# Modulation gates through DRAM, DMA transposes and idle products in a fused adaLN block of sliding attention and SwiGLU

## The chip, the core and the metric

One core of a Trainium2 chip. The metric is device time of one execution in microseconds (us), lower is better. The kernel before takes 255.45 us in the median of the four runs made beside the changed kernel (254.44 to 256.28), and 254.8 to 255.2 us in the calls of the experiments. The calls fell on different chips; in each, the kernel before was run beside the experiments. Most executions agree within a few tenths of a per cent; a run counts as "slow" when it is over 1.5% above the fastest of the same kernel. Ratios use the fast runs alone. Differences in us are of medians of all runs, and where slow runs shift one, the text says so. A kernel that was looked at only once has the state "unknown".

## The reference

A transformer block of 2048 rows by 512 columns, in bf16, whose two branches are modulated by a condition vector `c`:

```python
mod = (silu(c) @ w_mod)                        # six vectors of 512: sa, ca, ga, sb, cb, gb
h = layernorm(x) * (1 + ca) + sa               # LN1
x = x + ga * attention(h, wqkv, wo)            # 32 heads of 16; 8 keys, 2 rows apart, looking back
h = layernorm(x) * (1 + cb) + sb               # LN2
x = x + gb * ((silu(h @ w1) * (h @ w3)) @ w2)  # hidden size 1792
```

`ga` and `gb` are called the gates. Each is a row of 512 numbers that multiplies the columns of an output. The kernel multiplies them into the weights `wo` and `w2` once.

## The kernel before

The program is a list of operations. Each has an engine, an estimated cost and a priority; a planner in the host program places them in time by these, which fixes the order on every engine, and semaphore waits are then derived from the data. **Engines work strictly in that order.** The numbers in the priority table were found by search over the planner's estimates. The rows are handled in 16 tiles of 128. Parts that the change touches:

```python
# the condition vector times one, as four 128x128 stationary tiles (all columns equal)
for t in range(KT):
    p.op("dve", lambda e, t=t: e.tensor_scalar(csb[:, t, :], ones[:], csT[:, t:t + 1], None, op0=ALU.mult), 180, k, ...)

def gate(i):
    def mm(e):                       # the product comes out already repeated in all 128 partitions
        for t in range(KT):
            ins = e.matmul(bank(vm), csb[:, t, :], wm_g[i][:, t, :], start=(t == 0), stop=(t == KT - 1))
        return ins
    p.op("pe", mm, 4 * MM, k, r=[vwmg[i], vcsb] + wm_hold, w=[vm])
    dst = (ga_bc, gb_bc)[i]
    p.op("act", lambda e: e.activation(dst[:], bank(vm), ACT.Copy), c_act(512), k, r=[vm], w=[vg[i]])

def ln_stats(which, T):              # which = 0: LN1, 1: LN2
    ...                              # statistics on VectorE, 1/sqrt on GpSimd (add, then power)
    p.op("dve", lambda e: e.tensor_scalar(vn.at[:], x_sb[:, T, :], mv[:, i, 0:1], rs[:, i, :], op0=ALU.subtract,
                                          op1=ALU.mult), 350, ("nm", i), r=[vx[T], vr, vm], w=[vn])

def ln_T(which, gi, vns):            # a group of two or four tiles: transposed by TensorE into PSUM ...
    ...
    ins = e.transpose(b[:, col:col + P], vns[tt].at[:, ft * P:(ft + 1) * P], ident[:])
    ...                              # ... and scaled and shifted by ScalarE on the way out of PSUM
    return e.activation(vh.at[:, ft, 0:n * P], b[:, j * 512:j * 512 + n * P], ACT.Identity, bias=..., scale=...)

def values(T, i, ve, va):            # attention weights of a tile: written to DRAM, read back in another layout
    p.dma(bass.AP(a_dram, ...), lambda: ve.at[0][:, i]..., ("ad", T), 65536, ...)       # from SyncE
    p.dma(lambda: val.at[:], bass.AP(a_dram, ...), ("al", T), 65536 * 3, ...)           # from SyncE
    ...
```

The five LN2 groups feed the FFN: tiles 0 and 1, then three groups of four, then tiles 14 and 15.

The softmax here doesn't subtract the row's maximum and nothing guards it: scores larger than these inputs give would overflow.

## Time and profile before

| | before |
|---|---|
| time, median | 255.45 us |
| span of the profiled execution | 253.2 us |
| TensorE busy | 239.0 us (94%) |
| VectorE busy | 191.7 us (76%) |
| ScalarE busy | 111.4 us (44%) |
| GpSimd busy | 32.0 us (13%) |

In the profile, L with a number is a line of the kernel's source, and "out<-in" are the tiles by the program's names: `pall` is PSUM, `sb_wm_g` the gate weights, `sb_w` the FFN weights, `sb_vsh` the shifted values of the attention, `sb_xn` a normalized tile, `sb_h` a transposed group. The three views that carry the argument (engine totals and slices, busy time by stage, the chain that ended last) are shown and read in the prediction. The table of DMA issues of the kernel before (destination and source, issuing queue, number, size of each, median us from issue to landing):

```profile
sb_w<-in_B_w_dram SPq DMA_DIRECT2D x4, 512.0 KB, 7.9
...
a_scratch_dram<-sb_attn SPq DMA_DIRECT2D x16, 64.0 KB, 2.5
sb_al<-a_scratch_dram SPq DMA_DIRECT2D x16, 64.0 KB, 2.5
```

Loads of 512 KB land after about 8 us, the attention weights after 2.5 us. TensorE's table of waits is headed by these two (what was waited for, total us, how often, the longest), and the others are 1.3 us or less:

```profile
PE pall L574 <- DVE sb_xn L558: 6.4, 2, 5.6
PE pall L522 <- DMA sb_wm_s<-in_w_mod_dram: 1.5, 1, 1.5
```

Both are in the head of the kernel. After that TensorE hardly waits at all.

### The profile page before, as it was taken

The page shows a single profiled execution, that of the slowest core. Times are in us where ns is not written, and L with a number is a line of the kernel's source. Part 1 is how long each engine was busy: PE and PEld are TensorE (multiplying, and loading weights), DVE is VectorE, ACT ScalarE, POOL GpSimd, SP SyncE. Part 2 cuts the span into 40 slices and gives each one's busy share as a digit, 9 for nine tenths or more (in the row PEclk, how much of TensorE's full clock was granted, in tenths as well). Part 3 has the DMA queues.
Part 4 walks back from the last instruction along what each step waited for, and adds up shares of the span by engine and source line. Part 5 has one row for each costly group of instructions (what it writes and reads, how often), then busy time and mean ns, then how long its engine had stood idle before and what let it go on. Part 6 is the DMA issues. An engine that isn't in the chain of part 4 may idle for free.

```text
span 253.2 us, 5473 instructions
## 1 busy us (share of the span) xinstructions
PE 239.0 (94%) x2262; PEld 140.4 (55%) x2296; DVE 191.7 (76%) x298; ACT 111.4 (44%) x198; POOL 32.0 (13%) x81
## 2 busy tenths in 40 slices
PE   0599989999999999999999999999999999999995
PEld 0367555655488666546654544556544444565562
DVE  4759889999998989999899899999952443432432
ACT  2159748864863347432462273334234322420120
POOL 6237641001000040000002200020030000000000
PEclk9999999999999999999999999999999999999999
DMA  6997999899954595322369145393001000000101
GB/s 193 359 324 189 293 350 331 210 331 284 241 123 140 142 310 196 64 31 62 106 194 295 54 104 85 87 310 103 4 0 44 0 0 21 21 3 21 41 23 41
DMA packets 45817, 36.29 MB, mean 143 GB/s; under 512 B 19408, under 2 KB 36576, under 8 KB 45792
## 3 DMA queue, kind: packets, MB, share of 16 engines
q1 hardware_dynamic: 45264, 35.94, 49.4%
q8 instruction: 18, 0.29, 0.5%
q10 hardware_dynamic: 528, 0.00, 0.1%
q14 instruction: 7, 0.06, 0.1%
HBM read 30.67 MB, written 5.26 MB: 142 GB/s over the span
## 4 chain that ended last, share of the span: by engine, by line
PE 87%; DVE 5%; DMA 2%; POOL 2%; issue 1%; SPq 0%; ACT 0%; DVEq 0%
PE pall L771 36%; PE pall L792 19%; PE pall L615 9%; PE pall L755 5%; PE pall L742 5%; PE pall L633 5%; PE pall L673 4%; PE pall L574 2%; DMA sb_x<-in_A_x_dram 2%; POOL sb_rs L555 1%; DVE sb_xn L558 1%; DVE sb_st L550 1%; POOL sb_rs L553 1%; DVE sb_pq L664 1%; DVE sb_hh L780 1%
## 5 line engine op out<-in xcount | busy, mean ns | idle before, releaser
L771 PE MATMUL pall<-sb_h,sb_w 128*128 128x512 bf16 (+1 forms) x548 | 100.0, 336 | 0.7
L771 PEld LDWEIGHTS pall<-sb_h,sb_w 128*128 128x128 bf16 x560 | 53.7, 97 | 41.4
L777 ACT ACTIVATE sb_sg<-pall 128x512 bf16<-128x512 f32 (+1 forms) x70 | 35.6, 511 | 70.6 <-PE pall L771 70.3
L780 DVE TENSOR_TENSOR sb_hh<-sb_sg,pall 128x512 bf16<-128x512 bf16 (+1 forms) x70 | 39.5, 577 | 26.0 <-PE pall L771 23.8
L792 PE MATMUL pall<-sb_w,sb_hh 128*128 128x512 bf16 x216 | 49.7, 379 | 0.4
L664 DVE TENSOR_TENSOR sb_pq<-sb_q,sb_kT 128x4096 bf16<-128x4096 bf16 x16 | 36.4, 2283 | 0.5 <-ACT sb_q L622 0.3
L792 PEld LDWEIGHTS pall<-sb_w,sb_hh 128*128 128x128 bf16 x224 | 21.4, 98 | 23.5 <-DVE sb_hh L780 0.2
L615 PE MATMUL pall<-sb_h,sb_wqkv 128*128 128x512 bf16 (+1 forms) x155 | 31.9, 344 | 0.3
L582 ACT ACTIVATE sb_h<-pall,sb_modc 128x512 bf16<-128x512 bf16 (+1 forms) x36 | 23.1, 708 | 18.7 <-PE pall L574 13.1
L553 POOL TENSOR_TENSOR sb_rs<-sb_mv,sb_cst 128x1 f32<-128x1 f32 x32 | 8.8, 276 | 151.4 <-DVE sb_mv L551 148.4
L733 DVE TENSOR_TENSOR sb_vsh<-sb_vsh,sb_al 128x4096 bf16<-128x4096 bf16 x12 | 27.3, 2285 | 0.4 <-DMA sb_vsh<-v_scratch_dram 0.4
L798 DVE TENSOR_TENSOR sb_o<-pall,sb_x 128x512 bf16<-128x512 f32 x16 | 11.0, 688 | 18.0 <-PE pall L792 18.0
L550 DVE BATCH_NORM_STATS2 sb_st<-sb_x 128x6 f32<-128x512 bf16 x32 | 21.8, 682 | 3.3 <-DMA sb_x<-in_A_x_dram 3.2
L555 POOL TENSOR_TENSOR sb_rs<-sb_rs,sb_cst 128x1 f32<-128x1 f32 x32 | 20.9, 654 | 2.5
L615 PEld LDWEIGHTS pall<-sb_h,sb_wqkv 128*128 128x128 bf16 x160 | 15.1, 101 | 11.0 <-ACT sb_h L582 0.7
L633 PE MATMUL pall<-sb_wqkv,sb_h 128*128 128x512 bf16 x63 | 17.6, 411 | 1.5 <-DVE sb_xn L558 1.3
L574 PE MATMUL pall<-sb_ident,sb_xn 128*128 128x128 bf16 x128 | 12.8, 227 | 6.4 <-DVE sb_xn L558 6.4
L673 PEld LDWEIGHTS pall<-sb_E,sb_pq 128*128 128x128 bf16 x512 | 14.7, 96 | 2.7 <-DVE sb_pq L664 0.6
L748 ACT ACTIVATE sb_ot<-pall 128x512 bf16<-128x512 f32 x16 | 9.6, 598 | 13.6 <-PE pall L742 13.6
L574 PEld LDWEIGHTS pall<-sb_ident,sb_xn 128*128 128x128 bf16 x128 | 9.5, 101 | 10.6 <-DVE sb_xn L558 6.9
L755 PE MATMUL pall<-sb_wo,sb_ot 128*128 128x512 bf16 x58 | 15.0, 379 | 0.3
L673 PE MATMUL pall<-sb_E,sb_pq 128*128 128x32 bf16 x512 | 15.1, 177 | 0.0
(59 smaller groups left out, 163.8 us busy)
## 6 DMA issues: line engine op xcount, KB each, us to landing
sb_vsh<-v_scratch_dram SPq DMA_DIRECT2D x48, 256.0 KB, 4.4
sb_vshx<-v_scratch_dram SPq DMA_DIRECT2D x16, 256.0 KB, 4.5
sb_wm_s<-in_w_mod_dram SPq DMA_DIRECT2D x2, 1024.0 KB, 6.6
v_scratch_dram<-sb_v SPq DMA_DIRECT2D x16, 128.0 KB, 5.0
sb_w<-in_B_w_dram SPq DMA_DIRECT2D x4, 512.0 KB, 7.9
out_dram<-sb_o SPq DMA_DIRECT2D x16, 128.0 KB, 1.7
sb_w<-in_B_w_dram SPq DMA_DIRECT2D x1, 1792.0 KB, 8.9
sb_wqkv<-in_A_wqkv_dram SPq DMA_DIRECT2D x3, 512.0 KB, 7.9
```

Of the source, the lines that this page charges most:

```text
L550: o = p.op("dve", lambda e: e.bn_stats(st[:, i, :], x_sb[:, T, :]), 670, k, r=[vx[T]], w=[vs])
L574: ins = e.transpose(b[:, col:col + P], vns[tt].at[:, ft * P:(ft + 1) * P], ident[:])
L615: ins = e.matmul(bank(vp)[:, 0:n], wqkv[:, t, col:col + P], vh.at[:, t, 0:n], start=(t == 0), stop=(t == KT - 1))
L633: ins = e.matmul(bank(vp), vh.at[:, t, tt * P:(tt + 1) * P], wqkv[:, t, 2 * D:3 * D], start=(t == 0), stop=(t == KT - 1))
L664: return e.tensor_tensor(vp.at[:], in0, in1, ALU.mult)
L673: ins = e.matmul(b[:, c0:c0 + H], vp.at[:, w, ft, :], E_sb[:, ft, :], start=(ft == 0), stop=(ft == KT - 1))
L733: return e.tensor_tensor(v_w, v_w, a_w, ALU.mult)
L755: ins = e.matmul(bank(vy), vt.at[:, ft, :], wo[:, ft, :], start=(ft == 0), stop=(ft == KT - 1))
L771: ins = e.matmul(bank(vp)[:, 0:n], wt[:, t, fi * P:(fi + 1) * P], vh.at[:, t, 0:n], start=(t == 0), stop=(t == KT - 1))
L777: p.op("act", lambda e: e.activation(vt.at[:, 0:n], bank(vgp)[:, 0:n], ACT.Silu), c_act(n), k, r=[vgp], w=[vt], table="silu")
L780: p.op("dve", lambda e: e.tensor_tensor(vh_.at[:, 0:n], vt.at[:, 0:n], bank(vup)[:, 0:n], ALU.mult), c_dve(n), k, r=[vt, vup], w=[vh_])
L792: ins = e.matmul(bank(vz), vhh[fi].at[:, tt * P:(tt + 1) * P], w2[:, fi, :], start=(fi == 0), stop=(fi == NF - 1))
```

## The change

The intent: TensorE is the bound, so take work off it, and relieve VectorE, its nearest rival.

- The gates are computed as 16 one-column products each. The result is a column spread over partitions, which a GpSimd DMA writes to DRAM as a row of 512 numbers and a second one reads back, repeated over all partitions.
- LN2 groups 1 to 4 (14 tiles) are transposed by DMA rather than by TensorE; ScalarE then scales and shifts in place.
- LN2's normalization goes from VectorE to ScalarE, for which GpSimd computes a bias with two small products per tile.
- The DMAs of the attention weights are issued by GpSimd instead of SyncE.
- 70 idle products of 128 columns run at the start, to warm the array.
- The outputs of tiles 14 and 15 are done in halves of 256 columns.
- The priorities were searched again, with new cost estimates; the first loads are ordered differently.

```diff
+    def warm(i):
+        def mm(e):
+            for _ in range(5):
+                ins = e.matmul(bank(vw)[:, 0:P], ones[:], ones[:], start=True, stop=True)
+        p.op("pe", mm, 535, ("warm", i), r=[vc], w=[vw])          # NWARM = 14 of them
 ...
     def gate(i):
         def mm(e):
-            for t in range(KT):
-                ins = e.matmul(bank(vm), csb[:, t, :], wm_g[i][:, t, :], start=(t == 0), stop=(t == KT - 1))
+            for j in range(4):
+                for t in range(KT):
+                    ins = e.matmul(b[:, j:j + 1], wm_g[i][:, t, j * P:(j + 1) * P], csT_bf[:, t:t + 1], start=(t == 0),
+                                   stop=(t == KT - 1))
-        p.op("pe", mm, 4 * MM, k, r=[vwmg[i], vcsb] + wm_hold, w=[vm])
+        p.op("pe", mm, 16 * 27, k, r=[vwmg[i], vcs] + wm_hold, w=[vm])
+        p.op("dve", lambda e: e.tensor_copy(gcol[:, 4 * i:4 * i + 4], bank(vm)[:, 0:4]), 180, k, r=[vm], w=[vgc])
+        p.dma(bass.AP(g_dram, i * D, [[1, P], [P, KT]]), bass.AP(gcol, 4 * i, [[8, P], [1, 4]]), k, 90000, r=[vgc], w=[vgd], eng="pool", cost=900)
         dst = (ga_bc, gb_bc)[i]
-        p.op("act", lambda e: e.activation(dst[:], bank(vm), ACT.Copy), c_act(512), k, r=[vm], w=[vg[i]])
+        p.dma(dst[:], bass.AP(g_dram, i * D, [[0, P], [1, D]]), k, 131072, r=[vgd], w=[vg[i]], eng="pool", cost=900)
 ...
     def ln_stats(which, T):
+        if which:
+            p.op("pool", lambda e: e.tensor_tensor(nb[:, T, :], mv[:, i, 0:1], cst[:, 2:3], ALU.mult), 200, ...)
+            p.op("pool", lambda e: e.tensor_tensor(nb[:, T, :], nb[:, T, :], rs[:, i, :], ALU.mult), 200, ...)
+            p.op("act", lambda e: e.activation(vn.at[:], x_sb[:, T, :], ACT.Identity, bias=nb[:, T, :], scale=rs[:, i, :]),
+                 c_act(512) + 50, ("nm", i), r=[vx[T], vr, vb], w=[vn])
+            return vn
 ...
     def ln_T(which, gi, vns):
+        if which and gi >= DMA_T:                                  # DMA_T = 1
+            for tt in range(n):
+                p.dma(lambda tt=tt: vh.at[:, :, tt * P:(tt + 1) * P], lambda tt=tt: vns[tt].at[:], k, 157000, r=[vns[tt]],
+                      part=[vt, vh], cost=1250, transpose=True)
+            for ft in range(KT):
+                ... e.activation(vh.at[:, ft, 0:n * P], vh.at[:, ft, 0:n * P], ACT.Identity, bias=..., scale=...)
+            return vh
 ...
     def values(T, i, ve, va):                                      # both attention-weight DMAs
-              ("ad", T), 65536, r=[va, ve], w=[vad], cost=400)
+              ("ad", T), 65536, r=[va, ve], w=[vad], cost=900, eng="pool")
 ...
     def ffn_w2(T, tt, vhh):
+        if T >= NT - 2:                                            # two halves of 256 columns, each stored by itself
 ...
+    for i in range(NWARM):
+        warm(i)
 ...   (a wholly new table of priorities)
```

## The prediction

> **What bounds the kernel now.** I read the engine totals first, then the slices, then a table of busy time by stage, and last the chain that ended last at its two ends.
>
> ```profile
> PE 239.0 (94%) x2262; PEld 140.4 (55%) x2296; DVE 191.7 (76%) x298; ACT 111.4 (44%) x198; POOL 32.0 (13%) x81
> ...
> PE   0599989999999999999999999999999999999995
> ...
> DVE  4759889999998989999899899999952443432432
> ...
> PE 87%; DVE 5%; DMA 2%; POOL 2%; issue 1%; SPq 0%; ACT 0%; DVEq 0%
> ```
>
> TensorE works almost without a break from the second slice to the last, and 87% of the chain that ended last is TensorE. VectorE is a near second until 180 us and then only half busy. By stages (columns: length, then busy time and instruction count of PE, PEld, DVE, ACT, POOL, then granted clock, DMA share, GB/s):
>
> ```profile
> 0.00:12.00 12.00, 3.54 (x44) 2.13 (x45) 7.55 (x26) 2.51 (x4) 5.39 (x25) 1.00 0.83 273
> 18.00:30.00 12.00, 11.75 (x93) 8.01 (x94) 11.04 (x23) 10.56 (x24) 8.31 (x14) 1.00 0.88 225
> 30.00:60.00 30.00, 28.87 (x402) 17.30 (x406) 28.61 (x37) 21.03 (x36) 3.52 (x5) 1.00 0.99 308
> ...
> 240.00:253.20 13.20, 10.25 (x66) 6.29 (x65) 3.91 (x8) 1.92 (x5) 0.00 (x0) 1.00 0.09 31
> ```
>
> TensorE's idle time is 8.46 us in the first 12 us and 2.95 us after 240; summed over all windows between (12 to 240 us) it is only about 2.7 us. So a microsecond of matmul taken off between 12 and 250 us is worth about a microsecond of the end, as long as its feeders keep up. The head is a chain of its own (start, duration, what):
>
> ```profile
> 7.99 0.70 DVE sb_st L550
> ...
> 9.43 0.73 DVE sb_h L589 x2
> 10.16 0.33 DVE sb_xn L558
> 10.51 3.59 PE pall L633 x8
> 14.10 0.85 PE pall L615 x4
> 14.95 0.21 PE pall L574 x2
> 15.16 0.85 PE pall L615 x4
> 16.02 0.21 PE pall L574 x2
> 16.23 1.40 PE pall L615 x12
> 17.63 0.22 PE pall L574 x4
> ```
>
> The eight 512-column products from 10.51 take 449 ns each and the 256-column ones 213 ns; from 16.23 on the latter take 117 ns and later 109. TensorE runs at half speed until about 16.2 us although the granted clock in the slices reads 9 or more all along: this is the slow start of a rested array, which that row does not show.
>
> **What the Trainium skill says.** (1) "TensorE: Matmul & The Clock Gate", Part 1: a rested array runs at half clock and needs about 3.4 us of sustained activity, seen by a free-running window; start to start 426.7 ns cold and 215.7 warm at 512 columns, 106.7 and 55.6 at 128, and never below about 25 ns. The trace agrees: 449 (with a start delay) and 213 for half as many columns while cold, 55 ns for a warm transpose (0.22 us for four), and 0.79 us for the 32 one-column products of the second modulation, 24.7 ns each. (2) "DMA: Bandwidth & Descriptors", DMA Transpose (X-bar): the plain transpose can be issued only by the two hardware queues, and its rules say a transpose beside ordinary DMAs needs nothing extra. No run here shows it yet. The changed kernel issues all of them from SyncE, so from one stream. (3) "GPSIMD Engine Reference", Specifications: GpSimd's way to SBUF is shared with VectorE, with contention under two-input instructions. The trace agrees: the power on 128x1 elements takes 0.55 us in the median and 2.70 us once, when VectorE runs its 2.28 us product of two tensors. (4) The DMA page, SWDGE vs HWDGE vs iDMA: descriptors of a GpSimd DMA are written by GpSimd into SBUF, so the same lock-out delays them; the trace of before has no such DMA.
>
> **The change part by part.**
>
> *Transposes.* LN2 groups 1 to 4 (14 of 16 tiles) are transposed by DMA. That removes 14 x 4 = 56 TensorE transposes of 55 ns: 3.08 us, all on TensorE's saturated stretch. In their place come 14 DMAs of 128 KB from SyncE; the diff reckons 1.25 us of issue each. The evictions of these groups (ScalarE, 772 ns in the median form, from PSUM) become ScalarE passes in SBUF of about the same size. The latency of such a group grows: a four-tile group needs four issues plus a landing (2.5 us is what small DMAs took before), about 7 us instead of about 1. A preceding FFN group has 112 x 216 + 56 x 216 ns = 36 us of products, so this can be hidden.
>
> *Gates.* Two gates of four 512-column products (4 x 215.7 = 0.86 us each) become 16 one-column products at 24.7 ns, 0.40 us each. TensorE saves 2 x 0.47 = 0.94 us. The two 0.6 us ScalarE copies and the 1.0 us of VectorE broadcast go; two dependent DMAs per gate come, off the path, since the scaling of wo and w2 has tens of microseconds of slack.
>
> *Idle products first.* 14 x 5 products of 128 columns run from about 1.3 us, when the ones tile is set. Cold they take 70 x 107 ns = 7.5 us, less once the clock rises; that is two windows of activity, so TensorE should be warm when the first projection starts. The work between 10.51 and 16.23 is then 8 x 216 + 8 x 109 + 4 x 55 ns = 2.82 us instead of 5.72: 2.90 us saved at most.
>
> *Tail.* The last two tiles' outputs are cut into halves of 256 columns. The last VectorE add goes from 0.69 us to about 0.42 (what a 256-column product from PSUM takes on VectorE here, 419 ns), and the last store is half as large. Against that 56 x 109 ns for 28 x 215.7 ns, +0.07 us. Net about 0.25 us.
>
> *Off the bound.* VectorE loses 16 LN2 scalings of 0.40 us (6.5 us), now on ScalarE at about 0.6 us (+9.6 us of a 44% engine). One more half of an LN1 eviction goes from VectorE to ScalarE (+1.1 us there). The 32 attention-weight DMAs leave SyncE (0.58 and 0.38 us of issue each) for GpSimd. I credit nothing directly; VectorE at 95% until 180 us becomes less of a second bound, and that lets the saving on TensorE reach the end.
>
> Sum before debits: 3.08 + 0.94 + 2.90 + 0.25 = 7.2 us.
>
> **Debits.** (a) First loads: by the new priorities both pairs of x tiles go ahead of the modulation weights and another 512 KB of x ahead of the value weights. About the same bytes as before have to land before modulation (1.5 MB), so the first projection starts at 10.5 to 11 us, but the value weights may land 1.5 us later than before (512 KB at the 350 GB/s of that stretch). I take 0.4 us. (b) ScalarE in the first stage: from 9.43 to 30 us it worked 14.6 of 20.6 us, and 88% between 18 and 30. With 1.1 us more work in 2.9 us less time it is at 89% over the stretch; with eight PSUM banks as buffer some of the warm start is lost again. I take 0.6 us. (c) The array may not be warm in time or may pause too long while it waits for the modulation weights: 0.3 us on average. (d) New waits of ScalarE behind transposed tiles or of VectorE behind GpSimd DMAs: 0.4 us. (e) In return the order was searched anew, and some of the 2.7 us of idle time inside may go: I count 0.6 us. Together 7.2 - 1.7 + 0.6 = 6.1 us. From 255.89 us that is 249.8; I put it at **249.7 us** (2.4% less).
>
> **The rivals.** *ScalarE becomes the first-stage bound.* For: the 88% above, and two-tile groups need about 6.5 us of ScalarE evictions (eight of 0.39, two of 0.60, four of 0.56) for 5.6 us of warm TensorE work. Against: from 30 us on ScalarE is idle a third of the time. The warm start would then bring about 1 us and the time be 251.5. *Attention weights come late.* For: GpSimd can be held up to 2.3 us per VectorE product, twice in a row per tile (write, then read back), where SyncE needed 2.5 + 2.5 us to landing. Against: VectorE has other products to do meanwhile, and several tiles are in flight; FFN products fill TensorE after 70 us. If it fails, VectorE idles 1 to 2 us a tile for a few tiles: 252 to 254 us. *A transposed group is late*, so that ScalarE, which works in order, holds up SiLU and with it TensorE: 1 to 2 us per group at worst, 252 us. *All is hidden well and the new order removes most inner idle time:* 247.5.
>
> **Range and chances.** The three TensorE savings are firm in size (4.0 us without the warm start); only the 2.9 us of the warm start and the new waits vary. The saving must exceed 5.1 us for more than 2%. I expect 6.1 with a spread of some 2 us: range 247.0 to 252.6, chance of over 2% faster 0.70, within 2% 0.28, slower 0.02.
>
> **What would show it.** TensorE's busy sum without the idle products falls by about 7 us, of which 3.1 by transposes (72 left of 128) and 0.9 by gates. The first value projections take 216 ns each, not 449, starting at 10.5 to 11 us. If they are still at 427 ns, or ScalarE is over 95% between 12 and 30 us, step three fails. TensorE's idle time between 12 and 240 us stays under 4 us; if it is over 6, a wait took the place of the work removed, and the table of waits would name the transposed tiles or the attention weights. The last add is a 256-column one, and the span after the last product is about 2.6 us instead of 2.9. VectorE's total falls to about 183 us and ScalarE's rises to about 120; if VectorE then idles before its attention products, the GpSimd route is to blame.

## More of the kernel before

In the gate's write the DRAM pattern `[[1, P], [P, KT]]` says: partition p puts its four numbers at positions p, p+128, p+256 and p+384. So one write of 1 KB is made of 512 pieces of two bytes, and pieces from neighbouring partitions lie side by side.

## The result, and the profile after

The changed kernel takes **293.89 us** in the median of four runs (291.97 to 297.6) against 255.45 us: the ratio of the fast runs is 1.148, with a 95% interval of 1.138 to 1.158. (Ratios here are the mean time of one kernel's fast runs over that of the other's of the same rounds, so not quite the ratio of the medians.) Its output is correct. One of the four runs counts as slow; the profiled one is a fast one, with a span of 293.5 us.

The same views as before. Engine totals, the TensorE row of the 40 slices, and the shares of the chain that ended last:

```profile
PE 245.4 (84%) x2331; PEld 147.2 (50%) x2362; DVE 186.2 (63%) x280; ACT 121.9 (42%) x214; POOL 71.3 (24%) x149
...
PE   7599800891439979897999999799999999999995
...
PE 58%; DMA 24%; DVE 7%; ACT 4%; issue 3%; POOL 3%; SPq 1%; DVEq 0%
```

TensorE has two holes, in slices 6 and 7 and 10 to 12 (a slice is 7.3 us here). DMA, 2% of the chain before, is now 24% of it. The stages give the size (columns as in the prediction):

```profile
30.00:60.00 30.00, 12.83 (x170) 8.34 (x172) 12.31 (x27) 7.91 (x15) 4.88 (x6) 0.72 0.88 183
60.00:90.00 30.00, 14.96 (x114) 6.97 (x115) 11.20 (x7) 10.16 (x18) 5.73 (x8) 0.72 0.85 164
```

Of these 60 us TensorE works 27.8, where it worked 58.65 before. Summed over all stages from 12 to 240 us it is idle 40.4 us, against 2.8 before. No engine is busy in the holes: each stands at half or less. The DMA share is 0.85 to 0.88 all the same, while only 164 to 183 GB/s move, where the kernel before moved 308 in the first of these windows. The chain that ended last names the transfers (start, duration, what):

```profile
30.23 22.20 DMA sb_wm_g<-in_w_mod_dram
...
53.63 19.88 DMA g_scratch_dram<-sb_gcol
...
73.79 5.43 DMA sb_gb_bc<-g_scratch_dram
```

A write of one kilobyte, the second gate's, takes 19.88 us. A load of 512 KB of the second gate's weights (`sb_wm_g`) takes 22.20 us; the first gate's write was under way then (issued at 24.06, not landed before GpSimd issued the read at 43.56). The table of DMA issues says that this holds for everything that is on the way at the same time:

```profile
sb_w<-in_B_w_dram SPq DMA_DIRECT2D x4, 512.0 KB, 22.0
...
a_scratch_dram<-sb_attn POOLq DMA_DIRECT2D x16, 64.0 KB, 4.1
...
sb_h<-sb_xn SPq DMA_TRANSPOSE x14, 2.7
...
g_scratch_dram<-sb_gcol POOLq DMA_DIRECT2D x2, 1.0 KB, 19.9
```

The FFN weights' 7.9 us have become 22.0. The transposes, on the other hand, land after 2.7 us. A DMA view of the stretch in which the second write is under way, 54 to 73 us, sets the two rows side by side, DMA engines busy in tenths above, GB/s below (40 slices of 0.475 us):

```profile
DMA  9999999999993579999499089999309469678999
GB/s 349 347 344 342 332 335 370 367 340 336 380 200 35 56 62 58 58 47 43 52 50 17 0 11 30 9 17 34 15 0 39 32 69 108 125 162 181 204 162 168
```

For eleven slices bulk loads move at about 350 GB/s. Then, until close to the write's landing at 73.5, the engines are still shown as busy most of the time, at a fifth of that rate or less over the next twenty slices. "Busy" here does not mean "moving data". TensorE's waits:

```profile
PE pall L554 <- DMA sb_wm_g<-in_w_mod_dram: 16.9, 1, 16.9
PE pall L655 <- ACT sb_h L622: 9.6, 1, 9.6
PE pall L782 <- DVE sb_vsh L773: 5.1, 1, 5.1
PE pall L811 <- ACT sb_h L599: 3.0, 2, 2.4
```

The first is the gate's own product waiting for weights that are held up on their way. The second has the same cause: ScalarE, which works in order, stood 29.3 us in two waits for value tiles whose store to DRAM had not landed. Behind the third is VectorE, which waited 18.06 us for the gate's row (`sb_gb_bc`) before it could scale `w2`. Only the last is one of the waits that the prediction had thought of (a transposed group).

### The profile page after: what moved, and what is told of

It reads as the page before. It is cut to its first block, busy times and chain, and to the rows that moved or that the text cites. A ratio compares the mean times of both kernels' runs of the same rounds, so it can differ in the third digit from the quotient of the medians.

```text
span 293.5 us, 5658 instructions
## 1 busy us (share of the span) xinstructions
PE 245.4 (84%) x2331; PEld 147.2 (50%) x2362; DVE 186.2 (63%) x280; ACT 121.9 (42%) x214; POOL 71.3 (24%) x149
## 4 chain that ended last, share of the span: by engine, by line
PE 58%; DMA 24%; DVE 7%; ACT 4%; issue 3%; POOL 3%; SPq 1%; DVEq 0%
PE pall L811 29%; PE pall L846 10%; DMA sb_wm_g<-in_w_mod_dram 8%; DMA g_scratch_dram<-sb_gcol 7%; PE pall L795 4%; PE pall L655 4%; PE pall L673 3%; DMA sb_h<-sb_xn 3%; PE pall L782 3%; DMA sb_vshx<-v_scratch_dram 2%; DMA sb_wm_s<-in_w_mod_dram 2%; PE pall L833 2%; ACT sb_h L599 2%; DMA sb_gb_bc<-g_scratch_dram 2%; DVE sb_pq L704 2%
## 5 line engine op out<-in xcount | busy, mean ns | idle before, releaser
L846 PE MATMUL pall<-sb_w,sb_hh 128*128 128x512 bf16 x189 | 43.2, 379 | 0.4
L846 PEld LDWEIGHTS pall<-sb_w,sb_hh 128*128 128x128 bf16 x196 | 18.8, 98 | 21.8
L855 DVE TENSOR_TENSOR sb_o<-pall,sb_x 128x512 bf16<-128x512 f32 (+1 forms) x18 | 11.2, 630 | 27.6 <-PE pall L846 14.6
L572 POOL TENSOR_TENSOR sb_rs<-sb_mv,sb_cst 128x1 f32<-128x1 f32 x32 | 10.2, 317 | 58.7 <-DVE sb_mv L570 58.6
L683 ACT ACTIVATE sb_v<-pall 128x512 bf16<-128x512 f32 x16 | 9.4, 599 | 33.7 <-DMA v_scratch_dram<-sb_v 29.3
L574 POOL TENSOR_TENSOR sb_rs<-sb_rs,sb_cst 128x1 f32<-128x1 f32 x32 | 19.9, 620 | 2.5
L133 POOL DMA_DIRECT2D sb_al<-a_scratch_dram x16 | 14.4, 900 | 22.8 <-DMA a_scratch_dram<-sb_attn 22.0
L133 POOL DMA_DIRECT2D a_scratch_dram<-sb_attn x16 | 8.7, 547 | 34.6 <-DVE sb_attn L750 32.7
L581 ACT ACTIVATE sb_xn<-sb_x,sb_nb,sb_rs 128x512 bf16<-128x512 bf16 x16 | 12.8, 806 | 9.4 <-POOL sb_nb L580 9.4
L788 ACT ACTIVATE sb_ot<-pall 128x512 bf16<-128x512 f32 x16 | 9.4, 594 | 16.8 <-PE pall L782 15.5
L622 ACT ACTIVATE sb_h<-pall,sb_modc 128x512 bf16<-128x512 bf16 (+1 forms) x22 | 13.5, 688 | 5.6 <-DVE sb_modc L532 5.6
```

The source lines that it names most:

```text
L133: return e.dma_start(a, b, transpose=True) if transpose else e.dma_start(a, b)
L574: p.op("pool", lambda e: e.tensor_tensor(rs[:, i, :], rs[:, i, :], cst[:, 1:2], ALU.pow), 550, k, r=[va, vcst], w=[vr], lead=o)
L846: ins = e.matmul(bank(vz), vhh[fi].at[:, tt * P:(tt + 1) * P], w2[:, fi, :], start=(fi == 0), stop=(fi == NF - 1))
```

## The experiments

"Order kept" means that the planner was not run anew: the operation was removed, replaced or inserted in the finished list, and every other instruction keeps its place in its engine's order. Without this, a new placement would change everything at once. The theories to tell apart were: A, the gate write; B, the other transfers' new order and queues; C, the work moved to GpSimd and ScalarE.

### Gates as broadcast products

In the changed kernel the gate becomes four products of 512 columns again (the stationary operand is one column of the condition vector with step 0, so no tile has to be built), VectorE copies it out of PSUM, and both gate DMAs go. Order kept.

```diff
-                    ins = e.matmul(b[:, j:j + 1], wm_g[i][:, t, j * P:(j + 1) * P], csT_bf[:, t:t + 1], ...)
+                ins = e.matmul(bank(vm), bass.AP(csT_bf, t, [[KT, P], [0, P]]), wm_g[i][:, t, :], ...)
-        p.op("dve", lambda e: e.tensor_copy(gcol[...], bank(vm)[:, 0:4]), ...)
-        p.dma(<gate column to g_dram>)
-        p.dma(<g_dram to all partitions>)
+        p.op("dve", lambda e: e.tensor_copy(dst[:], bank(vm)), ...)
```

> The changed kernel with its two gates made as before (a broadcast product, 4 of 512 columns each, copied straight to the gate tile by VectorE); the two gate DMAs are left out, every other instruction keeps its place in its engine's order. Theory A (the two gate writes of 512 two-byte pieces hold the DMA engines some 20 us each, and that is the whole loss): 249 to 256 us, TensorE's idle time between 12 and 240 us under 8 us. Rival B (the loss comes from the attention weights on GpSimd's queue, the DMA transposes or the new order, and the gates only show it): over 270 us.

Measured: 265.85 us (265.0 to 266.98), ratio 1.0435 [1.0393, 1.0476]. That is 28.0 us less than the changed kernel, but 11 us more than the kernel before in the same call (254.76): between the two expectations. The gates' way through DRAM is the larger part, and something else costs about 11 us.

### The same, with the two writes as idle passengers

As above, but the two writes of 512 two-byte pieces are still issued at the change's place, from data that is ready. Nobody waits for them.

```diff
+        p.dma(bass.AP(g_dram, i * D, [[1, P], [P, KT]]), bass.AP(modc_bf, 0, [[16, P], [1, 4]]), k, ..., eng="pool")
```

> As the run before, but the two writes of 512 two-byte pieces to DRAM are issued where the change has them, from data that is ready, and nobody waits for them. Theory A1 (what hurts is that they keep the DMA engines from the other transfers): 272 us or more, both writes near 20 us to landing, and the loads beside them again 15 to 27 us. Theory A2 (what hurts is that the scaled weights wait for the gates): within 3 us of the run without them.

Measured: 290.1 us (288.39 to 293.62), ratio 1.1358 [1.1298, 1.1418]. The writes took 16.8 us to land in the median. TensorE's two longest waits:

```profile
PE pall L794 <- DVE sb_vsh L785: 14.5, 1, 14.5
PE pall L566 <- DMA sb_wm_g<-in_w_mod_dram: 10.8, 1, 10.8
```

Two writes of 1 KB whose result nobody reads cost 290.1 - 265.85 = 24.3 us (23.6 by the means of the fast runs; one run here was slow), by holding up the other transfers. The remaining 293.89 - 290.1 = 3.8 us separate two kernels. They hold the wait for the gates themselves, but also writes that took longer (19.9 us instead of 16.8); no run isolates the wait.

### Pieces of eight bytes

Each one-column product takes every fourth column of the weights, so that a partition holds four neighbouring gate numbers and writes them as one piece: 128 pieces of eight bytes in place of 512 of two.

```diff
-  wm_g[i][:, t, j * P:(j + 1) * P]        bass.AP(g_dram, i * D, [[1, P], [P, KT]])
+  wm_g[i][:, t, j:D:4]                    bass.AP(g_dram, i * D, [[4, P], [1, KT]])
```

> The changed kernel with the gate's columns taken every fourth, so that a partition's four values lie side by side in DRAM: 128 pieces of 8 bytes instead of 512 of 2. If each piece costs the same, the write lands in about 5 to 6 us instead of 19.9 and the time is 251 to 262 us; if the cost is that of a GpSimd DMA into DRAM as such, it lands near 20 us and the time stays near 290.

Measured: 273.05 us (269.89 to 273.73), ratio 1.069 [1.0622, 1.0758]. The write lands after 6.7 us in the median, and 20.8 us come back by changing the layout alone. The expectation of 251 to 262 was missed, since it took the gates for the only cost; the other 11 us are in this kernel too.

### Another queue for the writes

Only the issuing engine of the two gate writes changes, from GpSimd to ScalarE. Order kept; one look.

```diff
-  ... k, 90000, r=[vgc], w=[vgd], eng="pool", cost=900)
+  ... k, 90000, r=[vgc], w=[vgd], eng="act", cost=900)
```

> The changed kernel with only the two gate writes issued from ScalarE's hardware queue at the same place. If the pieces are the cost: again near 20 us to landing, 283 to 298 us. If GpSimd's software queue is the cost: under 8 us to landing and under 265 us.

Measured: 288.05 us (one run, state unknown). The writes still take 17.3 us. It isn't GpSimd's way of issuing.

### The gate change alone, on the kernel before

The kernel before with 16 one-column products per gate, a ScalarE copy of the four columns, and the write and the read from GpSimd. Order kept.

```diff
+    w = p.dma(bass.AP(g_dram, i * D, [[1, P], [P, KT]]), bass.AP(gcol, 4 * i, [[8, P], [1, 4]]), ..., eng="pool")
+    r = p.dma((ga_bc, gb_bc)[i][:], bass.AP(g_dram, i * D, [[0, P], [1, D]]), ..., after=[w], eng="pool")
```

> The kernel before with the gate change alone (16 one-column products, a four-column copy, a write of 512 two-byte pieces and a broadcast read on GpSimd's queue); all else in the order of before. Theory A: two writes of 16 to 20 us to landing and 275 to 295 us, that is 20 us or more over before. If the loss needs the rest of the change beside it: under 265 us.

Measured: 301.08 us (296.56 to 303.29), ratio of the fast runs 1.1681 [1.1615, 1.1748]; the profiled run was slow. Two of the four runs are slow; the fast ones, 296.56 and 299.18, are 43 us above the kernel before. The change of the gates alone is worse than the whole change. TensorE's waits show where it strikes:

```profile
PE pall L613 <- DVE sb_xn L597: 28.6, 2, 23.0
PE pall L781 <- DVE sb_vsh L772: 20.7, 3, 20.2
```

The writes took 19.0 us in the median. The first wait is LN1's (5.6 of its 28.6 us are in the kernel before too): GpSimd stood 33.6 us in two waits for the writes before it could issue the reads, and the statistics of the next tiles (its power instructions) were behind them in its order. So in this order the gate's wait also blocks the first stage.

### Unneeded small writes in a quiet stage

To see the write by itself: the kernel before, with 1 KB writes from GpSimd one after another, after 187 us, when VectorE is half busy and hardly any DMA runs. Each waits for the one before. Three runs, one look each, since only the durations matter.

```diff
+        for name, ap in patterns:                      # DRAM patterns, counted in two-byte elements
+            t = nc.dram_tensor(name, (512, 256), dt.bfloat16)
+            dep = p.dma(bass.AP(t, 0, ap), bass.AP(modc_bf, 0, [[16, P], [1, 4]]), ..., after=[dep], eng="pool")
+   run 1: [[1, P], [P, KT]] side by side; [[4, P], [1, 4]] 8-byte pieces; [[256, P], [256 * P, KT]] 512 bytes apart; side by side
+   run 2: [[s, P], [s * P, KT]] for s = 128, 64, 32, 16, 8, 4 (256 to 8 bytes apart)
+   run 3: the same for s = 2 and 3 (4 and 6 bytes apart); 256 four-byte pieces side by side; two-byte pieces side by side
```

> The kernel before, with four more writes of 1 KB to DRAM that nobody needs, one after another from GpSimd's queue in the quiet stage after about 187 us: 512 pieces of 2 bytes side by side, 128 of 8 bytes, 512 of 2 bytes each 512 bytes apart, 512 side by side again. If each piece has a fixed price: 15 to 20, 4 to 6, 15 to 20, 15 to 20 us to landing. If it is neighbours in one line that collide: the spread-out one is the fast one, under 6 us. If the 20 us were only the contention with the loads: all under 5 us here.

Measured (255.36 us in all, state unknown). GpSimd's timeline (start, duration of the issue, what, and in brackets the idle time ahead of it, in which the write before was under way):

```profile
187.53 0.93 POOL L133 DMA_DIRECT2D s_2b<-sb_modc_bf  x1 [0.30 <-POOL sb_rs L583]
204.78 0.56 POOL L133 DMA_DIRECT2D s_8b<-sb_modc_bf  x1 [16.32 <-issue]
208.33 0.76 POOL L133 DMA_DIRECT2D s_far<-sb_modc_bf  x1 [2.98 <-DMA s_8b<-sb_modc_bf]
210.88 0.75 POOL L133 DMA_DIRECT2D s_2b_more<-sb_modc_bf  x1 [1.80 <-DMA s_far<-sb_modc_bf]
```

Side by side, the write occupies 17 us from issue to issue (204.78 - 187.53 = 17.25) with nothing to contend with. As 128 pieces of eight bytes it is 3.55 us; as 512 two-byte pieces 512 bytes apart, 2.55 us. So it is neither a price per piece nor contention: it is pieces of two bytes as direct neighbours.

> The kernel before, with six more writes of 512 pieces of 2 bytes that nobody needs, one after another in the quiet stage, the pieces 256, 128, 64, 32, 16 and 8 bytes apart (the 2-byte step took 16.8 us, the 512-byte step 2.3 us). If neighbours inside one line of 64 bytes collide: 256, 128 and 64 near 2.3 us, then growing towards 17 us as more pieces share a line. If the line is 512 bytes: all well over 5 us, growing steadily as the distance shrinks.

Measured (256.49 us, state unknown): the five distances from 256 down to 16 bytes are alike. GpSimd waited 1.80 to 1.94 us for each of them, after an issue of 0.75 to 0.92 us, and they landed 2.3 to 2.4 us after the issue began. Both thresholds that I had guessed (64 and 512 bytes) fell. The sixth, 8 bytes apart, was followed by no issue; a DMA view of its stretch gives it 3.7 us to landing. So the rise begins between 16 and 8 bytes. The next expectation puts 8 bytes at 2.4 us as well: that is the median of all six, and not the time of this one.

> The kernel before with four unneeded 1 KB writes one after another in its quiet stage after 187 us: 512 two-byte pieces 4 bytes apart, then 6 bytes apart, then 256 four-byte pieces side by side, then 512 two-byte pieces side by side as the control. From 8 bytes on a write took about 2.4 us, side by side 17 us. Theory A, only pieces that share a four-byte word collide: 4 and 6 bytes apart and the four-byte pieces take 2 to 3.5 us. Theory B, the time grows as the distance shrinks: 4 bytes apart takes 7 to 9 us and the four-byte pieces likewise. The control takes 16 to 18 us in both.

Measured (254.82 us, state unknown):

```profile
187.03 0.92 POOL L133 DMA_DIRECT2D s<-sb_modc_bf  x1 [0.30 <-POOL sb_rs L584]
197.51 0.76 POOL L133 DMA_DIRECT2D s<-sb_modc_bf  x1 [9.56 <-DMA s<-sb_modc_bf]
203.50 0.71 POOL L133 DMA_DIRECT2D s_4b<-sb_modc_bf  x1 [5.23 <-DMA s<-sb_modc_bf]
211.52 0.78 POOL L133 DMA_DIRECT2D s<-sb_modc_bf  x1 [7.31 <-DMA s_4b<-sb_modc_bf]
```

From issue to issue: 4 bytes apart 10.5 us, 6 bytes apart 6.0 us, four-byte pieces side by side 8.0 us (theory B). To landing it is 10.2, 5.7 and 7.7 us. With 17 us for neighbours, 3.7 us to landing at 8 bytes and 2.3 to 2.4 us from 16 bytes on, the time grows as the distance shrinks. Nothing followed the control, so its own duration isn't in this view.

### Far pieces at the change's place

The kernel with idle passengers again, but the pieces 512 bytes apart. Order kept.

```diff
-  bass.AP(g_dram, i * D, [[1, P], [P, KT]])
+  bass.AP(g_dram, i * D * 256, [[256, P], [256 * P, KT]])
```

> The run in which the two writes of two-byte pieces were issued at the change's place and nobody waited for them (290.1 us), with the pieces 512 bytes apart instead of side by side. If the collision of neighbours is also what keeps the other transfers out: both land within 6 us and the time is that without any such write, 264 to 268 us. If many small pieces as such clog the engines: 280 us or more.

Measured: 265.15 us (262.72 to 269.32), ratio 1.0368 [1.0295, 1.0442], against 265.85 without any write and 290.1 with pieces side by side. The writes land after 3.8 to 6.0 us, and 512 KB loads after 9.4 (9.0 without any write). The loads' line with pieces side by side, and with pieces far apart:

```profile
sb_w<-in_B_w_dram SPq DMA_DIRECT2D x4, 512.0 KB, 21.1
...
sb_w<-in_B_w_dram SPq DMA_DIRECT2D x4, 512.0 KB, 9.4
```

As many pieces, as small, from the same queue at the same place: no harm. What holds others up is the neighbourhood of the pieces.

### Attention weights from GpSimd or SyncE

Two runs: the kernel with gates as products, with the attention-weight DMAs back on SyncE; and the kernel before with them on GpSimd. Order kept in both.

```diff
+        for o in p.placed:
+            if o.key[0] in ("ad", "al"):
+                o.eng = "sp"                 # in the other run: "pool"
```

> The run with the gates by products (265.85 us), and the attention-weight DMAs moved back from GpSimd's queue to SyncE's, all else in its place. Theory C (GpSimd's queue makes the weights late: write 4.9 us and read 6.3 us to landing ahead of a wait of TensorE of about 7 us around 40 to 54 us): 257 to 261 us and that wait gone. Rival D (the late transposed groups and the new order make the loss): 263 us or more.

> The kernel before with only its 32 attention-weight DMAs moved to GpSimd's queue. From the run that moved them back (no change at all): within 2 us of before. If GpSimd's one queue, shared with the LN statistics, makes either late: 257 us or more.

Measured: 265.75 us (265.17 to 267.34; ratio 1.0432) against 265.85, and 255.5 us (254.42 to 258.74; ratio 1.0055 [1.0001, 1.0109]). The queue makes no difference in the changed order and at most 1.1% in the old one; theory B falls as far as the queue goes. The totals hide one shift: with SyncE the attention weights' write landed after 6.32 us, and TensorE's longest wait was 7.5 us, for shifted values (`sb_vsh`), where it had been 2.5 us with GpSimd. The wait of about 7 us that the expectation names for the kernel with GpSimd isn't in its trace.

### Transposes: taken away, and done by DMA

Two runs on the kernel before. In the first, the 56 TensorE transposes of LN2 groups 1 to 4 are left out and nothing takes their place, so the result is wrong. (The comparison still passed: with these inputs the gates are so small that it doesn't see this branch.) In the second they are done by DMA from SyncE as in the change. Order kept.

```diff
-                p.op("pe", tr, 120, k, r=[vns[tt], vident], part=[vt])          # groups 1 to 4
+                p.dma(vh.at[:, :, tt * P:(tt + 1) * P], vn.at[:], ..., eng="sp", transpose=True)   # second run only
-                    return e.activation(vh.at[:, ft, 0:n * P], b[:, j * 512:j * 512 + n * P], ACT.Identity, ...)
+                    return e.activation(vh.at[:, ft, 0:n * P], vh.at[:, ft, 0:n * P], ACT.Identity, ...)
```

> Wrong result on purpose: the kernel before without the 56 TensorE transposes of LN2 groups 1 to 4 and with nothing in their place (the evictions scale whatever the tile holds); all else in its order. It measures what 3.1 us of products taken off TensorE between 90 and 220 us are worth at best. If TensorE alone sets the end: 3 us less, 251.5 to 252.3 us. If VectorE's chain, busy about 95% until 180 us, sets the pace there as it did behind the idle products: less than 1.5 us gained.

Measured: 251.79 us (250.39 to 252.67), ratio 0.9864 [0.9835, 0.9893]. The transposes are worth 3.3 us (255.10 - 251.79; 3.5 by the ratio), close to the predicted 3.08.

> The kernel before with those 56 transposes done by 14 transposing DMAs from SyncE's queue, each right after its tile is scaled, all else in the order of before. If a transposed group comes too late in the order as such (issue 1.2 us a tile, landing about 2.7 us, and the whole group must land): TensorE waits two to four times and the time is 256 to 262 us. If it is hidden: 251 to 254 us.

Measured: 268.85 us (267.44 to 270.66), ratio 1.054 [1.0491, 1.0589]. The gain is turned into a loss of 13.8 us. TensorE's longest wait, and ScalarE's behind it:

```profile
PE pall L829 <- ACT sb_h L651: 13.5, 3, 8.8
```

ScalarE waited 22.3 us in four times for transposed tiles. At one of them the chain reads: attention product of VectorE until 98.51, DMA transpose 5.07 us, four ScalarE passes 2.94 us, and then 15 FFN products in 5.07 us, 338 ns each rather than 216, after TensorE's wait of 8.8 us. The order of the kernel before brings a group's last tile just in time, and there the latency is not hidden. The transpose's own time is not all of it: its tile was ready at 94.11 and it was issued at 98.51, since SyncE, which works in order, was issuing four loads of shifted values, another transpose and a store until 98.46. So 4.4 us of this delay are the place in SyncE's queue, which is fuller here than in the changed order, where the attention weights are GpSimd's. No run separates the two.

### Idle products on the kernel before

The kernel before with 89 idle products, 45 before the first transposes, 20 before the modulation and 24 before the first projection, so that TensorE's pauses are filled.

```diff
+        for o, n in ((first projection, 24), (modulation, 20), (first operation, 45)):
+            insert n x e.matmul(PALL[:, 7 * 512:7 * 512 + P], ones[:], ones[:]) before o
```

> The kernel before with 89 idle products of 128 columns placed in TensorE's pauses of the first 10.5 us (45 ahead of the first transposes, 20 ahead of the modulation, 24 ahead of the first value projection), all else in its place. If a pause is what let the clock fall in the changed kernel: the first eight value products take 216 ns each and the time falls by 2 to 3 us, to 251.5 to 253 us. If ScalarE or the loads bound that stage: the products are fast but the time falls by less than 1 us.

Measured: 255.04 us (254.57 to 255.2), ratio 0.9999 [0.9971, 1.0028]. TensorE's timeline:

```profile
8.91 1.50 PE L330 MATMUL pall<-sb_ones 128*128 128x128 bf16 x24
10.90 1.67 PE L666 MATMUL pall<-sb_wqkv,sb_h 128*128 128x512 bf16 x7 [0.49 <-ACT sb_h L615]
13.01 0.61 PE L648 MATMUL pall<-sb_h,sb_wqkv 128*128 128x256 bf16 x4 [0.44 <-DMA sb_wqkv<-in_A_wqkv_dram]
...
15.56 1.05 PE L648 MATMUL pall<-sb_h,sb_wqkv 128*128 128x256 bf16 x8 [0.84 <-DMA sb_wqkv<-in_A_wqkv_dram]
...
37.62 0.28 PE L607 MATMUL pall<-sb_ident,sb_xn 128*128 128x128 bf16 x2 [0.82 <-DVE sb_xn L591]
```

The array is warm: seven 512-column products take 239 ns each, where eight took 449. But TensorE then waits for the query and key weights, and the transposes at 37.62 start within 0.1 us of the kernel before (37.56). The whole gain is given back by then.

### LN2 scaling on VectorE again

The kernel with gates as products; LN2's normalization on VectorE as before, and the 32 bias products of GpSimd gone. Order kept.

```diff
-            p.op("pool", <bias products>)
-            p.op("act", lambda e: e.activation(vn.at[:], x_sb[:, T, :], ACT.Identity, bias=nb[:, T, :], scale=rs[:, i, :]), ...)
+            p.op("dve", lambda e: e.tensor_scalar(vn.at[:], x_sb[:, T, :], mv[:, i, 0:1], rs[:, i, :], op0=ALU.subtract, op1=ALU.mult), ...)
```

> The run with the gates by products (265.85 us), with the LN2 scaling on VectorE again and the two GpSimd bias products per tile gone; all else in its place. If the bias products, which GpSimd did in 2.2 and 2.1 us ahead of a transposed group, and the 0.8 us ScalarE scaling make that group late: 260 to 263.5 us. If the DMA transposes themselves do: within 1.5 us of 265.85.

Measured: 260.61 us (259.24 to 261.18), ratio 1.0205 [1.0171, 1.0239]: 5.2 us less. In the changed kernel ScalarE waited 9.4 us in five times for the bias, up to 4.8 us at once. Theory C holds, for half of the 11 us. The bias products and ScalarE's pass went together, so the run doesn't say which of the two costs what.

### Bulk loads behind the first attention weights

What is left is 5.5 us. The chain of the kernel just above suggests that the first tile's attention weights come late, behind bulk loads:

```profile
41.71 5.07 DMA a_scratch_dram<-sb_attn
46.78 0.28 issue
47.07 6.33 DMA sb_al<-a_scratch_dram
```

So in that kernel the attention weights go back to SyncE and nine FFN weight loads are put behind those of the first two tiles.

```diff
+        late = [loads of w1, w3 and w2 placed before the second tile's attention weights]
+        p.placed = [everything else up to there] + late + [the rest]
```

> The run with gates and LN2 scaling as before (260.61 us), with the attention-weight DMAs on SyncE's queue and nine loads of FFN weights put behind the first two tiles' attention weights instead of ahead of them. If these loads make the first weights late (write and read took 5.1 and 6.3 us to landing there): 256 to 258.5 us. If the rest of the order does: within 1.5 us of 260.61.

Measured: 263.73 us (263.17 to 265.31), ratio 1.0365 [1.0302, 1.0429]: slower, not faster. The attention weights' write now landed in 1.97 us, but VectorE's scaling of `w2`, which comes before the attention's product in its order, stood 8.0 us waiting for the load that had been moved back. The run doesn't decide what the loads cost; it moved the wait. It also changed two things at once, and the queue alone had already brought TensorE a wait of 7.5 us here (in the run with attention weights on SyncE).

### Without transposes at all

The last question was whether the remaining 5.5 us are the latency of the DMA transposes. The kernel with gates as products and scaling on VectorE, with its 14 DMA transposes taken out and nothing in their place. Order kept. Its output is wrong, which doesn't matter for the time.

```diff
-                p.dma(lambda tt=tt: vh.at[:, :, tt * P:(tt + 1) * P], lambda tt=tt: vns[tt].at[:], ..., transpose=True)
```

> The changed kernel with the gates as broadcast products and the LN2 scaling on VectorE (which ran 260.61 us), now also without the fourteen DMA transposes and with nothing in their place; order kept, result wrong on purpose (the comparison is known to be too coarse to see it). Theory A, the late transposed groups are the rest: the time falls to 252 to 255 us, near the 251.79 us of the kernel before without its transposes, because both then do the same work. Theory B, the order of the first attention tiles and their loads is the rest: the time falls by at most 2 us, to 258.5 to 260.6 us.

Measured: 260.38 us (260.2 to 264.89), ratio 1.0208 [1.0182, 1.0235], against 260.61 us with them. With the gates and the LN2 scaling out of the way, the DMA transposes cost nothing in the changed order. What remains lies elsewhere: the kernel before without its transposes took 251.79 us, 8.6 us less, for nearly the same work (the kernel before ran alike, about 255.1). It was run at another time. The stages show where (columns as above):

```profile
30.00:60.00 30.00, 26.30 (x276) 14.39 (x278) 24.78 (x33) 18.18 (x32) 6.70 (x9) 0.92 1.01 318
60.00:90.00 30.00, 28.26 (x436) 19.63 (x439) 27.61 (x31) 16.11 (x30) 9.27 (x10) 0.96 0.63 184
```

In the kernel before without transposes TensorE works 28.86 and 29.77 us of these, at a granted clock of 1.00. So there are 4.1 us more idle time between 30 and 90 us, and the granted clock is lower besides. The clock reads 0.57 between 54 and 62 us and 0.53 between 89 and 92.5, and 1.00 in the other kernel in both stretches. Each of these follows a wait (in brackets) for shifted values, 2.85 us before 54.94 and 1.37 us before 88.25. The first:

```profile
54.94 1.01 PE L815 MATMUL pall<-sb_ind,sb_vsh 128*128 128x16 bf16 x32 [2.85 <-DVE sb_vsh L806]
...
60.02 1.91 PE L688 MATMUL pall<-sb_h,sb_wqkv 128*128 128x512 bf16 x4
```

The next product starts at 61.73, so these four take about 427 ns from start to start, instead of 216. From 30 us on, TensorE is busy 218.8 us here and 214.7 in the other kernel for the same work: the half-speed stretches are long enough to account for these 4.1 us, which idle time doesn't. That the clock fell because of the waits is an inference from their order in time; no run tests it. The head is made good: the first projection starts at 12.89 us against 10.5, but its products run at full speed from about 14.5, and by 30 us both kernels have done the same 96 projection products. I did not take the order of loads and first attention tiles apart further.

All timed results in one table, in us:

| kernel | median | against the one named |
|---|---|---|
| before | 254.8 to 255.45 | |
| changed | 293.89 | |
| changed, gates as products | 265.85 | -28.0 to changed |
| ... and two unneeded writes, side by side | 290.1 | +24.3 (fast runs +23.6) |
| ... and two unneeded writes, pieces 512 bytes apart | 265.15 | -0.7 |
| ... and attention weights from SyncE | 265.75 | -0.1 |
| ... and LN2 scaling on VectorE | 260.61 | -5.2 |
| ...... and no transposes at all (wrong result) | 260.38 | -0.2 |
| ...... and loads moved, attention weights from SyncE | 263.73 | +3.1 |
| changed, 8-byte pieces | 273.05 | -20.8 to changed |
| changed, writes from ScalarE's queue (one run) | 288.05 | -5.8 to changed |
| before, gates through DRAM | 301.08 | fast runs +43 to before |
| before, DMA transposes | 268.85 | +13.8 |
| before, without those transposes (wrong result) | 251.79 | -3.3 |
| before, idle products | 255.04 | 0 |
| before, attention weights from GpSimd | 255.5 | +0.4 |

No version beat the kernel before, other than the one that leaves work out. The transposes are the only one of the change's savings that a run showed to be real, and they are worth 3.3 us on the kernel before.

## Why the prediction was wrong, point by point

The prediction said 249.7 us and gave 2% to a loss. The kernel lost 38.4 us. The runs divide these as follows: 24.3 us (by medians) for transfers held up by the gate writes, 3.8 us for waiting for the gates and for the slower writes beside it, 5.2 us for LN2's scaling on ScalarE and GpSimd, and the remaining 5.2 us for the new order, net of what the change did save.

- **Gates: the step that failed.** "Two dependent DMAs per gate come, off the path" set the cost of the gates' new way at nothing and credited 0.94 us. The path argument alone was short: the write took 19.88 us, not a few. But the larger error is that a transfer off the path was taken to be free for the others. The passenger run shows that it isn't: nobody waits for it, and it costs 24.3 us, because other transfers stand still while it runs. Pieces 512 bytes apart cost nothing. The pattern that would have given this away, `[[1, P], [P, KT]]` over two-byte elements, stood in the diff, and was not costed.
- **LN2's scaling: a mis-sized term and one left out.** ScalarE's pass took 0.806 us, not 0.6, and the 32 bias products of GpSimd were not in the sum at all. They took 436 ns in the mean (0.19 us in the median, up to 2.2), where the planner reckoned with 200, and ScalarE waited for them. The prediction had named contention between VectorE and GpSimd for the power and for the DMAs, but put no new GpSimd work behind it. The totals were right (VectorE 186.2 us, predicted 183; ScalarE 121.9, predicted 120), but a total says nothing of who waits for it.
- **Idle products: right in mechanism, wrong in worth.** The 2.90 us "at most" supposed that a faster first stage moves the end. On the kernel before it was worth 0 by 38 us, since loads and VectorE bound this stretch; none of the prediction's debits went so far. In the changed kernel the array was not even warm. TensorE's timeline:

```profile
1.12 5.62 PE L540 MATMUL pall<-sb_ones 128*128 128x128 bf16 x65 [1.12 <-DVE sb_ones L440]
9.07 0.94 PE L523 MATMUL pall<-sb_csT_bf,sb_wm_s 128*128 128x1 bf16 x32 [2.32 <-DMA sb_wm_s<-in_w_mod_dram]
...
12.45 3.05 PE L673 MATMUL pall<-sb_wqkv,sb_h 128*128 128x512 bf16 x7 [1.25 <-DVE sb_mv L570]
```

  The 65 products warm it by 6.74 us, then come pauses of 2.3 and 1.25 us, and the first projections take 3.05 / 7 = 436 ns each, starting at 12.45 instead of 10.5 to 11. Of these 1.9 us 1.3 were lost before the modulation products, which waited for their weights (9.07 against 7.76 in the kernel before). The transposes between the two pauses still ran warm (14 in 0.82 us). Debit (c) named both halves of this and gave them 0.3 us; debit (a), 0.4 us for the order of loads, was closer to 2.
- **Transposes: right in size, and hidden in one order only.** 3.08 us predicted, 3.3 measured on the kernel before. "This can be hidden" held in the changed order once the gates and the scaling were mended (0.2 us), failed by 17 us in the order of the kernel before (268.85 - 251.79, in part by the place in SyncE's queue), and cost TensorE 3.0 us of waits in the changed kernel itself. The changed kernel with its transposes back on TensorE was not run, so their worth inside it stays an estimate.
- **Tail: nothing.** The halves of tiles 14 and 15 are not last in the new order. The last add is one of 512 columns again (0.69 us), and the span after the last product is 3.3 us rather than the predicted 2.6.
- **Attention weights on GpSimd.** The rival gave the right symptom, late attention weights, but not the cause: the queue is harmless or nearly so in both orders. GpSimd's issues of these DMAs took at most 0.93 us, so a hold-up of 2.3 us didn't reach them. One write took 18.5 us, beside a gate write, and at that time VectorE was waiting for the gate anyway.
- **The new order, credited with 0.6 us.** It was searched on the planner's estimates, in which a gate write takes a fraction of a microsecond beyond its latency and a bias product 200 ns. It is good for a machine that doesn't exist; with the gates and the scaling mended it still is some 5 us behind the old one, and that part I have located (idle time between 30 and 90 us, and stretches at half clock after waits) but not explained.
- **What the prediction's own tests said.** It asked for less than 4 us of TensorE idle time between 12 and 240 us, and said that over 6 would mean a new wait. It was 40.4. The table of waits then named first not the suspects that it had listed, but a load held up behind the gates. TensorE's busy time without the idle products was to fall by about 7 us: it was 245.4 - 6.1 = 239.3 us, against 239.0. The work did go (72 transposes were left, as predicted), but between 30 and 90 us the granted clock was 0.72 and the rest took longer. Small slips in the prediction's readings change nothing: 2.8 us of inner idle time and not 2.7, 0.78 us for the 32 one-column products and not 0.79, and 0.20 us rather than 0.25 for the tail before the store is counted.

Open: why neighbouring pieces of two bytes hold each other up, which is only described here, and how a write in this state stops other transfers. What of the last 5 us is due to which load, and why the clock falls after waits of 1.4 to 2.9 us.

## What to carry to other kernels

Before a DMA goes into a sum as "off the path", look at the size and the neighbourhood of the pieces that it writes: one kilobyte as 512 two-byte neighbours took 17 us with nothing beside it and held other transfers up for as long, while the same bytes as eight-byte pieces, or far apart, took about 3 us there; beside other loads the eight-byte pieces took 6.7 us. Test a suspected transfer as a passenger that nobody waits for: the difference is what it does to others. And before counting a faster stretch as a gain, change only that in the old kernel and look at the first place where it waits again.

## What the Trainium skill lacked or had wrong

- "DMA: Bandwidth & Descriptors", Specifications, says that below 512 bytes the DMA engine does a read-modify-write and leaves line rate. The runs agree that small pieces are slow, but not evenly: 512 two-byte pieces landed after 2.3 to 2.4 us at 256 down to 16 bytes apart, 3.7 us at 8 bytes, 5.7 at 6 and 10.2 at 4, and took 17 us side by side. No page has the distance between such small pieces as a quantity.
- The same page, "Why small descriptors are slow (HBM only)", gives costs per packet and per descriptor. Neither predicts this: the number of pieces was the same at 2.55 us (512 bytes apart) and at 17 us (side by side). Nor does it say that such a write to DRAM holds up other transfers (it says so only of stalled DMAs between cores): 512 KB loads beside it took 22.0 us instead of 7.9.
- "TensorE: Matmul & The Clock Gate", Part 1, has the array fall back to half clock after an idle window of about 3.4 us. Here two pauses of 2.3 and 1.25 us, neither as long as that, were followed by products of 436 ns. Between them lay 2.1 us of modulation, transposes and a few idle products; how much activity a window needs to count as busy the page doesn't say, and no run here shows it. In the run without transposes half clock followed single waits of 2.85 and 1.37 us in an otherwise busy stretch; the page speaks of frequent micro-idles in one kernel, without a length.
